# Cache loads on one ordered queue, a deeper K ring, and the output projection moved forward, in a decode kernel

## The chip, the cores and the metric

The kernel runs on one core of one Trainium2 chip. The metric is the device time of one execution in microseconds. A time is the median of several runs.

## The reference

One decode step for a batch of 2: attention of 16 query heads over a cache of 8 K/V heads with 32768 positions of 256 values, beside a small GELU feed-forward, mixed by a gate.

```python
q = (x @ wq).reshape(2, 1, 16, 256).transpose(0, 2, 1, 3)       # x is [2, 1, 448], bf16
k, v = repeat(k_cache, 2, axis=1), repeat(v_cache, 2, axis=1)   # caches [2, 8, 32768, 256], bf16
p = softmax(einsum("bhqd,bhkd->bhqk", q, k) / 16)
a = einsum("bhqk,bhkd->bhqd", p, v).transpose(0, 2, 1, 3).reshape(2, 1, 4096) @ wo
f = gelu(x @ w1 + b1) @ w2 + b2                                 # 448 -> 1792 -> 448
g = sigmoid((x * gate_w).sum(-1))
return g * a + (1 - g) * f
```

The two caches are 537 MB of the 547 MB that have to be read.

## The kernel before

There are 16 pairs (batch, K/V head), each with 16 K chunks and 16 V chunks of 1 MB (128 partitions x 16 tiles x 256). The scores of a whole pair are needed before its softmax, so the PV products of pair i run while the K chunks of pair i+1 are scored. A K chunk is transposed on the TensorE (PE) in four groups, copied out of PSUM by DVE or ACT, and multiplied by q; a V chunk takes 16 matmuls in four column groups, which leave four partial results.

K chunks live in a ring of NKB buffers and V chunks in a ring of NVB. SP issues K loads, ACT issues V loads, each on its own queue:

```python
def build_kernel(..., NKB=6, NVB=5, NKT=8, NTB=3, LAG=3):
    ...
    @block.sync
    def _(sp_):
        ...                                   # x, gate, biases; then all of wq, w1, w2
        for i in range(NP):
            for c in range(NCH):
                s, k = kslot(i, c)
                if k >= 1:
                    sp_.wait_ge(kfree[s], k)
                sp_.dma_start(knat[s][:, :, :], src).then_inc(kdma[s], 16)
        sp_.wait_ge(S["dve_fin"], 1)
        sp_.dma_start(out[:, 0, :], fin_bf[0:B, :])...
    ...
    def act_vtrig(i, c):                      # among ACT's other work, in order
        ...
        act.wait_ge(vfree[s], k)
        act.dma_start(vring[s][:, :, :], src).then_inc(vdma[s], 16)
```

The last pair's PV is followed by the combining of its four partials, a transpose, and the whole output projection in two halves of 224 columns:

```python
    def pe_attn_out(half):
        ...
        for h in range(HQ):
            for j in range(2):
                last = pe.matmul(ps[0:B, MB:MB + DHALF], lhsT=oT_bf[:, h, j, 0:B],
                                 rhs=wo_sb[:, h * 2 + j, half * DHALF:(half + 1) * DHALF], ...)
    def dve_a(half):
        ... tensor_copy(out=a_sb[half], in_=ps[0:B, MB:MB + DHALF])
        if half == 1:
            ... tensor_tensor(out=d1_sb, in0=a_sb, in1=f_sb, op=subtract)
            ... scalar_tensor_tensor(out=fin_bf, in0=d1_sb, scalar=g_sb, in1=f_sb, op0=mult, op1=add)
    ...
    ev(FIN, 4, "pe", "A0", pe_attn_out(0)); ev(FIN, 5, "dve", "A0r", dve_a(0))
    ev(FIN + 1, 4, "pe", "A1", pe_attn_out(1)); ev(FIN + 1, 5, "dve", "A1r", dve_a(1))
```

Of the kernel before, what the change touches and what calls it, by code (L numbers as in the profile page):

```python
# [4 lines left out]
ALU = mybir.AluOpType  # L5
# [49 lines left out]


def build_kernel(nc, A_x, A_k_cache, A_v_cache, A_wq, A_wo, B_x, B_w1, B_b1, B_w2, B_b2, gate_w, out,
                 NKB=6, NVB=5, NKT=8, NTB=3, LAG=3):
    B, _, D = A_x.shape
    _, HKV, SK, DH = A_k_cache.shape  # L60
    HQ = A_wq.shape[1] // DH
# [22 lines left out]
    def pair_bg(i):  # L84
        return i // HKV, i % HKV

    def drows(dc):
        return min(128, D - dc * 128)
# [80 lines left out]
    def kslot(i, c):  # L169
        gi = i * NCH + c  # L170
        return gi % NKB, gi // NKB

# [44 lines left out]
    with nc.Block() as block:  # L217
# [44 lines left out]
        def _(pool_):  # L262
# [7 lines left out]
            ch(pool_.memset(ones_f[:], 1.0))  # L270
            assert ch.n == POOL_DONE

        @block.sync
        def _(sp_):
            sp_.dma_start(x_bf[0:B, :], A_x[:, 0, :]).then_inc(S["ldA"], 16)
            sp_.dma_start(gw_bf[0:B, :], bass.AP(gate_w.tensor, gate_w.offset, [[0, B], [1, D]])).then_inc(S["ldA"], 16)
            sp_.dma_start(b2_bf[0:B, :], bass.AP(B_b2.tensor, B_b2.offset, [[0, B], [1, D]])).then_inc(S["ldA"], 16)
            sp_.dma_start(b1_sb[0:NFC, :], B_b1.rearrange("(c p) -> c p", p=128)).then_inc(S["ldA"], 16)
            for dc in range(NDC):
                r = drows(dc)  # L280
                wqv = vring[dc][:, :, :].rearrange("p t d -> p (t d)")
                sp_.dma_start(wqv[0:r, :], A_wq[dc * 128:dc * 128 + r, :]).then_inc(S["ld_wq"], 16)
            for dc in range(NDC):
                r = drows(dc)
                sp_.dma_start(w1_sb[0:r, dc, :], B_w1[dc * 128:dc * 128 + r, :]).then_inc(S["ld_w1"], 16)
            sp_.dma_start(w2_sb[:, :, :], B_w2.rearrange("(c p) d -> p c d", p=128)).then_inc(S["ld_w2"], 16)
            for i in range(NP):
                b, g = pair_bg(i)
                for c in range(NCH):
                    s, k = kslot(i, c)  # L290
                    if k >= 1:
                        sp_.wait_ge(kfree[s], k)
                    src = A_k_cache[b, g, c * C:(c + 1) * C, :].rearrange("(p t) d -> p t d", p=128)
                    sp_.dma_start(knat[s][:, :, :], src).then_inc(kdma[s], 16)
            sp_.wait_ge(S["dve_fin"], 1)
            sp_.dma_start(out[:, 0, :], fin_bf[0:B, :]).then_inc(S["osem"], 16)
            sp_.wait_ge(S["osem"], 16)

        def pe_prologue():
            pe.wait_ge(S["pool_c"], POOL_DONE)  # L300
            pe.wait_ge(S["ldA"], 16 * N_LDA)
            pe.wait_ge(S["dve_init"], 1)
            misc_begin("XT")
            last = None
            for dc in range(NDC):
                r = drows(dc)
                col = MB + 2 * dc
                last = pe.matmul(ps[0:r, col:col + 2], lhsT=x_bf[0:B, dc * 128:dc * 128 + r],
                                 rhs=identb[0:B, 0:B], start=True, stop=True)
            misc_end(last)  # L310
            misc_begin("B1T")
            last = pe.matmul(ps[:, MB:MB + NFC], lhsT=b1_sb[0:NFC, 0:128], rhs=identb[0:NFC, 0:NFC],
                             start=True, stop=True)
            misc_end(last)
            misc_begin("Q")
            pe.wait_ge(S["ld_wq"], 16 * NDC)
            last = None
            for h in range(HQ):
                for j in range(2):
                    col = MB + (h * 2 + j) * 2  # L320
                    for dc in range(NDC):
                        r = drows(dc)
                        wqv = vring[dc][:, :, :].rearrange("p t d -> p (t d)")
                        last = pe.matmul(ps[:, col:col + 2],  # L324
                                         lhsT=wqv[0:r, h * DH + j * 128:h * DH + j * 128 + 128],
                                         rhs=xT_sb[0:r, dc, 0:B], start=(dc == 0), stop=(dc == NDC - 1))
            misc_end(last)
            misc_begin("HT")
            pe.wait_ge(S["ld_w1"], 16 * NDC)
            last = None  # L330
            for fc in range(NFC):
                for dc in range(NDC):
                    r = drows(dc)
                    last = pe.matmul(ps[:, MB + 2 * fc:MB + 2 * fc + 2],  # L334
                                     lhsT=w1_sb[0:r, dc, fc * 128:(fc + 1) * 128],
                                     rhs=xT_sb[0:r, dc, 0:B], start=(dc == 0), stop=(dc == NDC - 1))
            misc_end(last)
# [16 lines left out]
        def pe_attn_out(half):  # L354
# [16 lines left out]
                    pass  # L371
            return fn

        def pe_tr(n):
            def fn():
                i, rem = divmod(n, G)
# [4 lines left out]
                if n >= NTB:  # L381
# [3 lines left out]
                    else:  # L385
                        pe.wait_ge(S["ev_dve"], evac_count(m))
                tb = tbank(n)
                last = None
                for tl in range(4):
                    t = 4 * q + tl  # L390
                    for j in range(2):
                        blk = tl * 2 + j
                        last = pe.transpose(tb[:, blk * 128:(blk + 1) * 128],  # L393
                                            knat[s][:, t, j * 128:(j + 1) * 128], identb[:, :])
                if evac_eng(n) == "act":
                    v = tr_act.inc(last)
                    assert v == evac_count(n)
                else:
                    v = tr_dve.inc(last)
                    assert v == evac_count(n)  # L400
# [13 lines left out]
        def pe_qk(n):  # L414
            def fn():
# [17 lines left out]
                for tl in range(4):  # L433
                    t = 4 * q + tl
                    col = base + (c * T + t) * 2
                    for j in range(2):
# [3 lines left out]
                                         start=(j == 0), stop=(j == 1))  # L440
                        if first is None:
                            first = last
                if pending_kfree:
                    assert len(pending_kfree) == 1
                    first.then_inc(kfree[pending_kfree.pop()], 1)
                last.then_inc(ktfree[slot], 1)
# [214 lines left out]
                                             in1=f_sb[0:B, :], op0=ALU.mult, op1=ALU.add).then_inc(S["dve_fin"], 1)  # L661
            return fn

        def act_vtrig(i, c):
            def fn():
                b, g = pair_bg(i)
                s, k = vslot(i, c)
                if k >= 1:
                    act.wait_ge(vfree[s], k)
                elif s < NWQ:  # L670
                    act.wait_ge(S["pe_misc"], misc_k("Q") + 1)
                src = A_v_cache[b, g, c * C:(c + 1) * C, :].rearrange("(p t) d -> p t d", p=128)
                act.dma_start(vring[s][:, :, :], src).then_inc(vdma[s], 16)  # L673
            return fn

        def act_wo():
            act.dma_start(wo_sb[:, :, :], A_wo.rearrange("(c p) d -> p c d", p=128)).then_inc(S["ld_wo"], 16)

        def act_gate():
            act.wait_ge(S["dve_gz"], 1)  # L680
# [19 lines left out]

        PRO = -1000
        ev(PRO, 0, "pe", "PRO", pe_prologue)
        misc_names.extend(["XT", "B1T", "Q", "HT"])
        ev(PRO - 1, 0, "dve", "INIT", dve_prologue_init)
        ev(PRO, 5, "dve", "XTr", dve_xt)
        ev(PRO, 6, "dve", "B1Tr", dve_b1t)
        ev(PRO, 7, "dve", "Qr", dve_q)
        ev(PRO, 8, "dve", "HTr", dve_ht)
        for i in range(NP):
            for c in range(NCH):  # L710
                a = vtrig_anchor(i, c)
                _, k = vslot(i, c)
                if k == 0:
                    ev(PRO + i * NCH + c, 12, "act", f"V{i},{c}", act_vtrig(i, c))
                else:
                    ev(a, 12, "act", f"V{i},{c}", act_vtrig(i, c))
        ev(PRO + NP * NCH + 1, 12, "act", "WO", act_wo)
        ev(PRO + NP * NCH + 2, 8, "act", "GATE", act_gate)
        ev(PRO + NP * NCH + 3, 8, "act", "GELUT", act_gelu_tanh)
        FA = min(8, NG)  # L720
        ev(FA, 5, "dve", "GELU2", dve_gelu2)
        ev(FA + 1, 4, "pe", "F0", pe_ffn_f(0))
        misc_F = [("F0", FA + 1), ("F1", FA + 2)]
        ev(FA + 1, 5, "dve", "F0r", dve_f(0))
        ev(FA + 2, 4, "pe", "F1", pe_ffn_f(1))
        ev(FA + 2, 5, "dve", "F1r", dve_f(1))
        for n in range(NG):
            ev(n, 0, "pe", f"tr{n}", pe_tr(n))
            if n % GPC == GPC - 1:
# [3 lines left out]
        for i in range(NP):  # L733
# [11 lines left out]
            ev(oc_anchor[i], 3, "dve", f"OC{i}", dve_ocomb_step(i))  # L745
            ev(oc_anchor[i] + 1, 4, "pe", f"OT{i}", pe_otr(i))
            ev(oc_anchor[i] + 1, 5, "dve", f"OTr{i}", dve_ot_step(i))
        ev(FIN, 4, "pe", "A0", pe_attn_out(0))
        ev(FIN, 5, "dve", "A0r", dve_a(0))
        ev(FIN + 1, 4, "pe", "A1", pe_attn_out(1))  # L750
        ev(FIN + 1, 5, "dve", "A1r", dve_a(1))

        events.sort(key=lambda e: (e[0], e[1], e[2]))
        for e in events:
            if e[3] == "pe" and (e[4].startswith(("TRM", "BC", "RS", "OT", "F0", "F1", "A0", "A1"))):
                misc_names.append(e[4])

        @block.tensor
        def _(pe_):
# [46 lines left out]
```

## Time and profile before

| | before |
|---|---|
| time, median of 4 runs | 1354.92 us (1354.38 to 1355.18) |
| span of the profiled run | 1353.1 us |
| HBM bytes read | 547.43 MB |
| PE busy | 78% |
| last V chunk landed | 1335.8 us |
| from there to the end | 17.3 us |

The page's queue table of the kernel before has packets, bytes and the share of the sixteen DMA engines' time, by queue. q1 is SP's queue, q10 is ACT's:

```profile
q1 hardware_dynamic: 39740, 275.34, 49.2%
q10 hardware_dynamic: 40976, 272.12, 49.1%
q8 instruction: 165, 2.70, 0.8%
```

Together the two load queues, q1 and q10, are 98% of the sixteen engines' time. The chain of waits on the same page, by engine, agrees:

```profile
DMA 78%; PE 16%; DVE 3%; issue 2%; ACTq 1%; ACT 0%; SPq 0%; DVEq 0%
```

The table by stretches of the kernel before: after the window and its length come PE, PE weight load, DVE, ACT and POOL busy time with instruction counts, the granted clock, the DMA share, and GB/s.

```profile
0.00:30.00 30.00, 15.09 (x202) 13.60 (x203) 2.86 (x11) 1.49 (x2) 1.41 (x9) 1.00 0.93 332
...
400.00:600.00 200.00, 160.67 (x3198) 142.94 (x3199) 80.93 (x137) 57.01 (x65) 0.00 (x0) 0.82 1.01 416
600.00:800.00 200.00, 158.30 (x3178) 142.21 (x3174) 78.84 (x128) 56.25 (x62) 0.00 (x0) 0.83 1.01 417
...
1270.00:1300.00 30.00, 23.41 (x492) 20.74 (x489) 13.55 (x24) 8.57 (x11) 0.00 (x0) 0.85 0.92 356
1308.00:1328.00 20.00, 8.18 (x128) 3.00 (x128) 0.00 (x0) 0.00 (x0) 0.00 (x0) 0.50 1.01 423
```

Mid-run the engines are full (share 1.01) at 416 to 417 GB/s, and PE is not. From 1308 to 1328 us only V's queue has work, and the rate is no lower. The list of waits of the kernel before (who waited for whom: us in total, times, longest) says which data PE runs out of:

```profile
PE ps L529 <- DMA vring<-in_A_v_cache_dram: 223.6, 197, 3.2
...
PE pst L393 <- DMA knat<-in_A_k_cache_dram: 2.0, 1, 2.0
```

It is V almost always. Last, the end of the timeline of the kernel before (start, duration, engine, line, operation; in brackets the idle time before it and what ended it):

```profile
1335.79 1.02 PE L529 MATMUL ps<-vring,p_sb 128*2 128x256 bf16 x16 [1.41 <-DMA vring<-in_A_v_cache_dram]
1336.87 0.41 DVE L636 COPY o_tmp<-ps 2x256 f32<-2x256 f32 x1 [35.99 <-PE ps L529]
1337.32 1.32 DVE L638 TENSOR_TENSOR o_tmp<-o_tmp,ps 2x256 f32<-2x256 f32 x3
1338.67 0.34 DVE L640 TENSOR_SCALAR o_sb<-o_tmp,rrec 2x256 f32<-2x256 f32 x1
...
1340.49 5.58 PE L365 MATMUL ps<-wo_sb,oT_bf 128*2 128x224 bf16 x32 [0.35 <-DVE oT_bf L649]
1346.10 0.38 DVE L656 COPY a_sb<-ps 2x224 f32<-2x224 f32 x1 [5.76 <-PE ps L365]
...
1346.54 3.23 PE L365 MATMUL ps<-wo_sb,oT_bf 128*2 128x224 bf16 x32 [0.47 <-DVE a_sb L656]
1349.80 0.38 DVE L656 COPY a_sb<-ps 2x224 f32<-2x224 f32 x1 [3.32 <-PE ps L365]
1350.21 0.61 DVE L659 TENSOR_TENSOR d_sb<-a_sb,f_sb 2x448 f32<-2x448 f32 x1
1350.86 0.67 DVE L660 SCALAR_TENSOR_TENSOR fin_bf<-d_sb,g_sb,f_sb 2x448 bf16<-2x448 f32 x1
```

No transfer of size runs here any more (0 GB/s from 1336 to 1340 us, 2 GB/s from 1340 to 1350). The step from 1340.5 to 1350.2 us is the output projection, and 14 of its 16 heads were ready 40 us earlier.

### The profile page before, as it was taken

To read this page: it belongs to the slowest core of one execution; us is meant where nothing else is said; L and a number is where in the kernel's file an instruction comes from. 1 tells how busy PE (TensorE), PEld (TensorE's weight loads), DVE (VectorE), ACT (ScalarE), POOL (GpSimd) and SP (SyncE) were. 2 spreads that over 40 slices of the span, in tenths; PEclk is the share of its full clock that TensorE was granted. 3 is DMA by queue.
4 is the path that set the end of the run, shared out by engine and by line. 5 is a ranking of instruction groups with operands and counts; after the bars stand their busy time and mean duration, and the time that the engine had idled before them with its cause. 6 is when DMAs were issued, how large, how long until landed. Compare 5 with 4: busy or idle time off the path is not lost.

```text
span 1353.1 us, 45118 instructions
## 1 busy us (share of the span) xinstructions
PE 1059.7 (78%) x20921; PEld 940.9 (70%) x20921; DVE 527.7 (39%) x890; ACT 367.3 (27%) x408; POOL 1.4 (0%) x9
## 2 busy tenths in 40 slices
PE   4986787878877887878787778788788878877865
PEld 4876676877767776767777677677677767777742
DVE  1553443434334343343434334343343434334321
ACT  0333232222323233232323223232232222222210
POOL 0000000000000000000000000000000000000000
PEclk9998987777888788788878878888788778878866
DMA  9999999999999999999999999999999999999994
GB/s 342 416 413 415 419 420 419 419 419 420 419 419 418 419 420 419 418 403 420 406 419 420 418 417 401 420 415 420 415 404 420 407 419 420 419 419 416 387 381 169
DMA packets 80904, 550.36 MB, mean 407 GB/s; under 512 B 8388, under 2 KB 14284, under 8 KB 14732
## 3 DMA queue, kind: packets, MB, share of 16 engines
q1 hardware_dynamic: 39740, 275.34, 49.2%
q10 hardware_dynamic: 40976, 272.12, 49.1%
q8 instruction: 165, 2.70, 0.8%
q14 instruction: 23, 0.19, 0.0%
HBM read 547.43 MB, written 0.00 MB: 405 GB/s over the span
## 4 chain that ended last, share of the span: by engine, by line
DMA 78%; PE 16%; DVE 3%; issue 2%; ACTq 1%; ACT 0%; SPq 0%; DVEq 0%
DMA vring<-in_A_v_cache_dram 76%; PE pst L393 8%; PE ps L529 4%; PE ps L438 2%; DMA knat<-in_A_k_cache_dram 1%; DVE o_tmp L638 1%; DMA vring<-in_A_wq_dram 1%; ACTq L673 1%; PE ps L324 1%; PE ps L365 1%; PE ps L511 1%; DVE o_tmp L636 0%; PE ps L334 0%; DVE pm_sb L596 0%; DVE kT L471 0%
## 5 line engine op out<-in xcount | busy, mean ns | idle before, releaser
L393 PE MATMUL pst<-identb,knat 128*128 128x128 bf16 x8192 | 759.8, 247 | 18.9 <-ACT kT L468 8.2
L471 DVE COPY kT<-pst 128x1024 bf16<-128x1024 bf16 x683 | 465.7, 691 | 725.1 <-PE pst L393 723.6
L393 PEld LDWEIGHTS pst<-identb,knat 128*128 128x128 bf16 x8192 | 568.6, 111 | 86.4 <-issue 76.2
L468 ACT ACTIVATE kT<-pst 128x1024 bf16<-128x1024 bf16 x341 | 349.2, 1024 | 844.9 <-PE pst L393 833.9
L438 PE MATMUL ps<-qT_sb,kT 128*128 128x2 bf16 x8192 | 367.8, 166 | 3.0 <-issue 2.0
L529 PE MATMUL ps<-vring,p_sb 128*2 128x256 bf16 x4096 | 184.8, 307 | 225.5 <-DMA vring<-in_A_v_cache_dram 223.6
L438 PEld LDWEIGHTS ps<-qT_sb,kT 128*128 128x128 bf16 x8192 | 347.5, 102 | 4.5 <-issue 4.5
L529 PEld LDWEIGHTS ps<-vring,p_sb 128*2 128x2 bf16 x4096 | 80.6, 87 | 267.5 <-DMA vring<-in_A_v_cache_dram 250.2
L695 ACT ACTIVATE p_sb<-ps,nb_sb 128x256 bf16<-128x256 f32 x32 | 16.5, 542 | 56.5 <-DVE nb_sb L615 56.5
L511 PE MATMUL ps<-identf,o_sb 2*128 2x2 f32 x64 | 13.0, 303 | 20.2 <-DVE nb_sb L615 17.8
L511 PEld LDWEIGHTS ps<-identf,o_sb 2*128 2x128 f32 x64 | 11.6, 253 | 21.8 <-DVE nb_sb L615 19.0
L636 DVE COPY o_tmp<-ps 2x256 f32<-2x256 f32 x16 | 6.5, 406 | 38.2 <-PE ps L529 38.2
L638 DVE TENSOR_TENSOR o_tmp<-o_tmp,ps 2x256 f32<-2x256 f32 x48 | 20.0, 416 | 1.7
L324 PE MATMUL ps<-xT_sb,vring 128*128 128x2 bf16 (+1 forms) x128 | 9.2, 174 | 10.8 <-DMA vring<-in_A_wq_dram 10.8
L324 PEld LDWEIGHTS ps<-xT_sb,vring 128*128 128x128 bf16 (+1 forms) x128 | 8.3, 106 | 11.8 <-issue 10.9
L481 PE MATMUL ps<-identf,pm_sb 128*2 128x128 f32 x32 | 6.6, 290 | 6.2 <-DVE pm_sb L596 6.2
L596 DVE TENSOR_REDUCE pm_sb<-ps 128x2 f32<-128x512 f32 x16 | 10.9, 680 | 0.9 <-PE ps L438 0.9
L365 PE MATMUL ps<-wo_sb,oT_bf 128*2 128x224 bf16 x64 | 8.8, 312 | 0.8 <-DVE a_sb L656 0.5
L681 ACT ACT_TABLE_LOAD x1 | 1.3, 1283 | 27.0 <-issue 27.0
L365 PEld LDWEIGHTS ps<-wo_sb,oT_bf 128*2 128x2 bf16 x64 | 6.3, 101 | 3.1 <-DVE a_sb L656 0.7
L554 DVE CAST qT_sb<-ps 128x64 bf16<-128x64 f32 x1 | 0.4, 435 | 19.9 <-PE ps L324 19.9
L490 PE MATMUL ps<-dg_sb,ones_f 2*128 2x2 f32 x32 | 7.1, 288 | 0.2 <-DVE dg_sb L605 0.2
(45 smaller groups left out, 62.7 us busy)
## 6 DMA issues: line engine op xcount, KB each, us to landing
knat<-in_A_k_cache_dram SPq DMA_DIRECT2D x256, 1024.0 KB, 20.8
vring<-in_A_v_cache_dram ACTq DMA_DIRECT2D x256, 1024.0 KB, 23.5
wo_sb<-in_A_wo_dram ACTq DMA_DIRECT2D x1, 3584.0 KB, 86.7
vring<-in_A_wq_dram SPq DMA_DIRECT2D x3, 1024.0 KB, 6.9
w_sb<-in_B_w_dram SPq DMA_DIRECT2D x1, 1568.0 KB, 17.2
w_sb<-in_B_w_dram SPq DMA_DIRECT2D x3, 448.0 KB, 12.1
vring<-in_A_wq_dram SPq DMA_DIRECT2D x1, 512.0 KB, 11.4
w_sb<-in_B_w_dram SPq DMA_DIRECT2D x1, 224.0 KB, 13.7
```

The costliest lines, as they stand in the source:

```text
L324: last = pe.matmul(ps[:, col:col + 2], lhsT=wqv[0:r, h * DH + j * 128:h * DH + j * 128 + 128], rhs=xT_sb[0:r, dc, 0:B], start=(dc == 0), s ...
L365: last = pe.matmul(ps[0:B, MB:MB + DHALF], lhsT=oT_bf[:, h, j, 0:B], rhs=wo_sb[:, h * 2 + j, half * DHALF:(half + 1) * DHALF], start=(k2 = ...
L393: last = pe.transpose(tb[:, blk * 128:(blk + 1) * 128], knat[s][:, t, j * 128:(j + 1) * 128], identb[:, :])
L438: last = pe.matmul(ps[:, col:col + 2], lhsT=kT[slot][:, blk * 128:(blk + 1) * 128], rhs=qT_sb[:, b, j, REP * g:REP * g + 2], start=(j == 0 ...
L468: ins = act.activation(out=kT[slot][:, :], in_=tbank(n), func=ACT.Copy)
L471: ins = dve.tensor_copy(out=kT[slot][:, :], in_=tbank(n))
L511: last = pe.matmul(ps[:, MB + 2 * j:MB + 2 * j + 2], lhsT=o_sb[0:2, si, j * 128:(j + 1) * 128], rhs=identf[0:2, 0:2], start=True, stop=True)
L529: last = pe.matmul(ps[32 * gq:32 * gq + 2, base:base + 256], lhsT=p_sb[:, i, (c * T + t) * 2:(c * T + t) * 2 + 2], rhs=vring[s][:, t, :], ...
L596: v = dve_pm.inc(dve.tensor_reduce(out=pm_sb[:, 2 * si:2 * si + 2], in_=scv, axis=AX.X, op=ALU.max))
L638: dch(dve.tensor_tensor(out=o_tmp[0:2, :], in0=o_tmp[0:2, :], in1=ps[32 * gq:32 * gq + 2, base:base + 256], op=ALU.add))
L673: act.dma_start(vring[s][:, :, :], src).then_inc(vdma[s], 16)
L695: v = act_exp.inc(act.activation(out=pv[:, m, :], in_=scv[:, m, :], func=ACT.Exp, bias=nb_sb[:, 2 * si + m:2 * si + m + 1], scale=SCALE, a ...
```

## The change

Its intent is threefold: to give K and V one order of loading that follows the order in which PE frees their buffers, with two more K buffers; to take work out of the start; and to take the output projection out of the end. Cut to its core:

```diff
-                 NKB=6, NVB=5, NKT=8, NTB=3, LAG=3):
+                 NKB=8, NVB=5, NKT=8, NTB=3, LAG=3):
...
+        # one job per K and V chunk; "a" is the step at which its buffer comes free
+        early = [j for j in jobs if j["a"] is None]
+        late = [j for j in jobs if j["a"] is not None]
+        late.sort(key=lambda j: (j["a"], j["u"]))
+        for j in early + late:
+            q = "sp" if load["sp"] <= load["act"] else "act"
+            if j["a"] is not None:
+                q = "sp"                      # all of the steady state on SP's queue
...
-            for dc in range(NDC): ...         # wq, w1, w2, then all K loads, on SP
+            for dc in WQ_SP:                  # half of wq on SP, half on ACT
+                load_wq(sp_, dc)
+            ...                               # then the jobs; w1, w2 after the eighth; wo on ACT
...
-        ev(PRO, 7, "dve", "Qr", dve_q)        # Q, HT and the FFN leave the prologue
+        ev(QA, 4, "pe", "Q", pe_q)
+        ev(HA, 4, "pe", "HT", pe_ht)
...
-        ev(FIN, 4, "pe", "A0", pe_attn_out(0))
-        ...
+        for h in range(HQ - REP):             # 14 heads, one after each of the last pair's V chunks
+            ev(pv_anchor(NP - 1, 1 + h), 12, "pe", f"PA{h}", pe_ap(h))
+        ev(FIN, 4, "pe", "PF", pe_af)         # the last pair's two heads: 4 matmuls, 448 wide
+        ev(FIN, 5, "dve", "PFr", dve_af)      # reads the result from PSUM, no copies
```

The release of a K buffer also moves, from the next score matmuls to the next transposes.

## The prediction

> **What bounds the kernel now.** The DMA engines. By the page's queue table the two load queues take 49.2% and 49.1% of the sixteen engines' span, 550.36 MB. The chain of waits is 78% DMA, 76% loads of V. The table by stretches shows 412 to 419 GB/s at a DMA share of 1.00 to 1.02 in every stretch from 30 to 1250 us. PE is busy 78%; its own waits are almost all for V (223.6 us), slack that the transfers leave.
>
> The last V chunk lands at 1335.8 us. At the mid-run pace of about 416 GB/s, 550 MB take 1323 us, and transfers start at about 3.4 us; the small-row weights (278 to 369 GB/s at 14 to 20 us) and a dip at 1276 to 1296 us (about 316 to 356) account for most of the rest. So almost nothing idles before 1335.8 us. The remaining tail is 17.3 us: PV 1.05, combining four PV partials 2.3, transposing the result and waits 1.3, the output projection in two halves 9.7 (1340.5 to 1350.2), two DVE steps 1.3, store and end 1.6.
>
> **What the change does.**
> 1. 28 of the 32 projection products, now 448 wide, move between the PV chunks of the last pair, where PE waits 1.4 us of every 2.48 us for V. After the last V only 4 remain. A 224-wide one takes 0.174 us there (5.58/32), so 4 of double width are about 1.4 us (estimate), without the copies between halves. **-8.3 us, all on the critical path.**
> 2. All steady K and V loads go on SP's queue in one order. No bandwidth gained: at 1308 to 1328 us only the V queue works, at 420 to 426 GB/s, as much as two together.[...] The waits follow PE's order of releases, so I expect no head-of-line loss: 0 to +2 us.
> 3. K buffers 6 to 8. PE waited only 2 us for K; the V ring of 5 limits. But K ends sooner, leaving V alone with 5 chunks in flight across the last softmax (about 7 us without a release): 0 to +2 us.
> 4. Wq first on both queues, HT and FFN out of the prologue, W1/W2 deferred: the dip at 12 to 20 us is partly filled: -1 us at most, since bytes bound this stage.
> 5. V issues leave ACT, where one blocks 10.8 us at 96.6 us in the chain; off the bound, 0.
> 6. The K release moves to the next transposes: 0.
>
> **Prediction: 1346 us**, range 1340 to 1351; faster by over 2%: 0.03, within 2%: 0.94, slower by over 2%: 0.03.
>
> **What would show it.** Last V landing at 1334 to 1338 us; from there to the end about 9 us; the two projection halves gone from the end of the timeline. ACT's queue down to a dozen issues, SP's near 97% of the engines' span. Mid-run 414 to 420 GB/s, share 1.0. PE still waiting 200 us or more for V, next to nothing for K; V's issue to landing still about 22 us.
>
> **What would make it wrong.** If the single ordered queue starves the engines (share under 0.97 mid-run), or SP's wait for Q (about 27 us) leaves a hole at 30 to 60 us, it is slower. If mid-run dips such as 575 to 585 us (349 to 377 GB/s) come from order or buffer depth and go, up to 9 us (1250 us at 416 instead of 419.5) more is gained: about 1337. If the last softmax starves V, the end dip grows and eats part of the gain.

## More of the kernel before

Each experiment ran in one job, on one chip, with runs of the kernel before, and its ratio is formed against those.

## The result, and the profile after

The changed kernel takes 1345.66 us (median of 9 runs, 1345.27 to 1346.60) against 1354.50 us (13 runs) of the kernel before: ratio 0.9934, 95% interval 0.9925 to 0.9944. Here and below a ratio is the mean time of one kernel's runs over that of the other's runs of the same rounds, so it is not quite the ratio of the medians quoted. The profiled span fell from 1353.1 to 1343.5 us, by 9.6 us.

The queue table of the changed kernel:

```profile
q1 hardware_dynamic: 75804, 538.03, 97.1%
q10 hardware_dynamic: 4912, 9.44, 2.0%
q8 instruction: 164, 2.69, 0.8%
```

The traffic has moved to one queue as intended, and it takes the same engine time: 99.1% of a span that is 0.7% shorter. The same stretches:

```profile
0.00:30.00 30.00, 6.76 (x81) 6.26 (x81) 2.74 (x7) 2.51 (x3) 1.41 (x9) 1.00 0.96 365
...
400.00:600.00 200.00, 157.97 (x3177) 142.09 (x3178) 80.88 (x137) 56.37 (x64) 0.00 (x0) 0.84 1.01 419
600.00:800.00 200.00, 161.35 (x3170) 145.00 (x3169) 78.17 (x127) 56.32 (x61) 0.00 (x0) 0.80 1.01 417
...
1270.00:1300.00 30.00, 24.17 (x507) 21.20 (x502) 13.71 (x25) 9.27 (x12) 0.00 (x0) 0.81 0.91 338
1308.00:1328.00 20.00, 12.46 (x150) 4.71 (x144) 0.00 (x0) 0.00 (x0) 0.00 (x0) 0.66 1.01 422
```

The start is fuller (365 instead of 332 GB/s), the dip before the last softmax is a little deeper (338 instead of 356), and the middle is what it was: the mean of all 5 us windows from 25 to 1275 us is 415.9 GB/s, against 416.3 before. The waits of the changed kernel:

```profile
PE ps L637 <- DMA vring<-in_A_v_cache_dram: 221.8, 195, 3.2
...
PE pst L496 <- DMA knat<-in_A_k_cache_dram: 24.3, 2, 14.7
```

PE still waits for V in the middle. Its two waits for K stand at the start: 14.7 us until 23.8 us, for the first K load, and 9.6 us until 68.3 us. Before the second, SP had stood 16.1 us at one V issue (39.6 to 55.7 us), and the K loads in line behind that issue went out late. And the end:

```profile
1334.70 0.61 PE L637 MATMUL ps<-vring,p_sb 128*2 128x256 bf16 x16 [0.99 <-DMA vring<-in_A_v_cache_dram]
1335.36 0.41 DVE L744 COPY o_tmp<-ps 2x256 f32<-2x256 f32 x1 [35.05 <-PE ps L637]
1335.81 1.32 DVE L746 TENSOR_TENSOR o_tmp<-o_tmp,ps 2x256 f32<-2x256 f32 x3
1337.16 0.34 DVE L748 TENSOR_SCALAR o_sb<-o_tmp,rrec 2x256 f32<-2x256 f32 x1
...
1338.88 1.65 PE L466 MATMUL ps<-wo_sb,oT_bf 128*2 128x448 bf16 x4 [0.26 <-DVE oT_bf L757]
...
1340.57 0.61 DVE L472 TENSOR_TENSOR d_sb<-ps,f_sb 2x448 f32<-2x448 f32 x1 [1.74 <-PE ps L466]
1341.22 0.67 DVE L473 SCALAR_TENSOR_TENSOR fin_bf<-d_sb,g_sb,f_sb 2x448 bf16<-2x448 f32 x1
```

The last V lands at 1334.7 us, 1.1 us earlier, and 8.8 us follow it instead of 17.3. So 8.5 us of the 9.6 come from behind the last transfer.

The trace also holds the completion time of every 1 MB cache load, and the n-th completion of one kernel can be set against the n-th of the other. This is worked out from the completion records, not a view of the profile:

```
cache load, from 0        10     40    100    250    400    490    511
before, us              54.8  139.0  292.6  674.0 1055.4 1283.2 1335.8
after, us               46.9  137.0  290.5  672.1 1053.4 1281.2 1334.7
difference               7.9    2.0    2.0    2.0    2.0    2.0    1.1
```

Up to load 10 the order of the weights differs. The columns from load 40 to 490 are loads that land second of a K and a V load. Their difference is 1.8 to 2.1 us in 217 of 226 cases, so over 1.1 ms the loads land at the same pace. The loads between them differ by 2.7 to 4.4 us, because before the change the two loads of a pair land 0.1 to 1.8 us apart and after it about 2.5 us. By all bytes landed, the changed kernel leads by 1.0 us from 60 to 200 MB, by 2.4 to 3.6 us from 250 to 525 MB, and by 1.1 us at 540 MB, after the dip before the last softmax. So both counts leave 1.1 us at the end, and both lose in the dip, but whether the start gained 1 or 2 us depends on the count, and each kernel has one profile.

### The profile page after: what moved, and what is told of

Same layout as the page of the kernel before. It is cut to its first block, busy times and chain, and to the rows that moved or that the text cites. A ratio compares the mean times of both kernels' runs of the same rounds, so it can differ in the third digit from the quotient of the medians.

```text
span 1343.5 us, 45053 instructions
## 1 busy us (share of the span) xinstructions
PE 1047.1 (78%) x20889; PEld 929.6 (69%) x20889; DVE 526.4 (39%) x888; ACT 367.5 (27%) x408; POOL 1.4 (0%) x9
## 3 DMA queue, kind: packets, MB, share of 16 engines
q1 hardware_dynamic: 75804, 538.03, 97.1%
## 4 chain that ended last, share of the span: by engine, by line
DMA 80%; PE 14%; DVE 2%; SPq 2%; issue 2%; ACT 0%; DVEq 0%
DMA vring<-in_A_v_cache_dram 78%; PE pst L496 7%; PE ps L637 4%; DMA knat<-in_A_k_cache_dram 2%; PE ps L546 2%; SPq L328 1%; DVE o_tmp L746 1%; PE ps L397 1%; PE ps L619 1%; DVE pm_sb L704 0%; PE ps L409 0%; DVE o_tmp L744 0%; PE ps L589 0%; SPq L351 0%; PE ps L466 0%
## 5 line engine op out<-in xcount | busy, mean ns | idle before, releaser
L496 PE MATMUL pst<-identb,knat 128*128 128x128 bf16 x8192 | 751.7, 246 | 26.9 <-DMA knat<-in_A_k_cache_dram 24.3
L496 PEld LDWEIGHTS pst<-identb,knat 128*128 128x128 bf16 x8192 | 562.3, 110 | 94.4 <-issue 65.3
L637 PE MATMUL ps<-vring,p_sb 128*2 128x256 bf16 x4096 | 182.1, 303 | 222.9 <-DMA vring<-in_A_v_cache_dram 221.8
L619 PEld LDWEIGHTS ps<-identf,o_sb 2*128 2x128 f32 x64 | 11.1, 243 | 22.8 <-DVE nb_sb L723 20.2
L457 PE MATMUL ps<-wo_sb,oT_bf 128*2 128x448 bf16 x28 | 11.3, 500 | 0.0
L598 PEld LDWEIGHTS ps<-dg_sb,ones_f 2*128 2x128 f32 x32 | 5.6, 219 | 0.8 <-DVE dg_sb L713 0.5
## 6 DMA issues: line engine op xcount, KB each, us to landing
vring<-in_A_v_cache_dram SPq DMA_DIRECT2D x256, 1024.0 KB, 24.1
```

Source lines behind the costliest of these rows:

```text
L457: pe.matmul(ps[0:B, SC[0]:SC[0] + D], lhsT=oT_bf[:, h, j, 0:B], rhs=wo_sb[:, h * 2 + j, :], start=(h == 0 and j == 0), stop=False)
L496: last = pe.transpose(tb[:, blk * 128:(blk + 1) * 128], knat[s][:, t, j * 128:(j + 1) * 128], identb[:, :])
L598: ins = pe.matmul(ps[:, MB:MB + 2], lhsT=ones_f[0:2, 0:128], rhs=dg_sb[0:2, 2 * si:2 * si + 2], start=True, stop=True)
L619: last = pe.matmul(ps[:, MB + 2 * j:MB + 2 * j + 2], lhsT=o_sb[0:2, si, j * 128:(j + 1) * 128], rhs=identf[0:2, 0:2], start=True, stop=True)
L637: last = pe.matmul(ps[32 * gq:32 * gq + 2, base:base + 256], lhsT=p_sb[:, i, (c * T + t) * 2:(c * T + t) * 2 + 2], rhs=vring[s][:, t, :], ...
```

## The experiments

The theory under test (A) is: the transfers run at a pace that neither queue, order nor K depth touches, and the change gains what it takes from behind the last V, with 1 to 2 us from the start. The first rival (B) credits the ordered queue and the deeper ring. Each experiment gave the correct result.

### The tail alone

The kernel before, with only the projection moved:

```diff
# against the kernel before
-        ev(FIN, 4, "pe", "A0", pe_attn_out(0)) ... dve_a(1)
+        for h in range(HQ - REP):
+            ev(pv_anchor(NP - 1, 1 + h), 12, "pe", f"PA{h}", pe_ap(h))
+        ev(FIN, 4, "pe", "PF", pe_af); ev(FIN, 5, "dve", "PFr", dve_af)
```

> The kernel before, with only the output projection moved: 28 of its 32 products, 448 wide, run between the last pair's V chunks, and 4 stay behind the last V. Theory A (the change gains by its tail): the last V lands at 1335 to 1336.5 us as before, the tail after it falls from 17.3 to about 8.8 us, and the time is 8 to 9 us below before, ratio 0.9934 to 0.9941. Rival B (the ordered queue and the deeper K ring gain, the tail little): at most 3 us below before, ratio 0.998 or more.

Measured: 1346.56 us against 1355.66, ratio 0.9937 (0.9923 to 0.9950). The first matmul on the last V chunk, from its timeline:

```profile
1335.57 1.02 PE L556 MATMUL ps<-vring,p_sb 128*2 128x256 bf16 x16 [1.47 <-DMA vring<-in_A_v_cache_dram]
```

The span was 1344.7 us, so 9.2 us follow the last V. The tail alone gives nearly all of the gain; B is rejected.

### Everything but the tail

```diff
# against the changed kernel
-        for h in range(HQ - REP): ev(..., pe_ap(h)); ev(FIN, ..., pe_af); ev(FIN, ..., dve_af)
+        ev(FIN, 4, "pe", "A0", pe_attn_out(0)) ... dve_a(1)
```

> The changed kernel with the old projection at its end (two halves after the last V); queue order, 8 K buffers, start and K release stay as changed. Theory A: the last V lands at about 1334.7 us as in the changed kernel, the tail is 17.3 us again, ratio to before 0.998 to 1.000 (0 to 2 us gained by the start). Rival B: ratio 0.994 to 0.996, most of the gain remains.

Measured: 1353.73 us, ratio 0.9989 (0.9976 to 1.0001), last V at 1335.3 us, 16.9 us behind it. Queue, order, ring, start and release together are worth about 0.1%, which the interval (a gain of 0.24% to a loss of 0.01%) does not tell from nothing. The two parts add up: 0.63% and 0.11% against 0.66% for the whole change, within the intervals.

### V back on ACT's queue

```diff
# against the changed kernel
             if j["a"] is not None:
-                q = "sp"
+                q = "act" if j["kind"] == "V" else "sp"
```

> The changed kernel with the V loads of the steady state issued by ACT again, on ACT's queue, at the same places in the order of work; everything else as changed. Theory A (which queue carries a load is nothing to the sixteen engines): ratio to before 0.9925 to 0.9945, as the changed kernel, and mid-run about 416 GB/s. Rival B (one ordered queue is worth something): 2 us or more slower than the changed kernel, ratio 0.995 or more.

Measured: 1346.36 us, ratio 0.9933 (0.9921 to 0.9945), last V at 1335.3 us. Two queues or one is the same here, to the resolution of the runs. The queue tables of the two kernels fit this: the two load queues took 49.2% and 49.1% of the sixteen engines' time before, and after the change SP's queue alone took 97.1%.

### Six K buffers

```diff
# against the changed kernel
-                 NKB=8, NVB=5, ...
+                 NKB=6, NVB=5, ...
```

> The changed kernel with 6 K buffers instead of 8. Theory A: V's ring of 5 holds the pace, so ratio to before 0.9925 to 0.9945, equal to the changed kernel; PE waits for K stay under 30 us in total and the end dip before the last softmax is smaller (K ends later). Rival B (the two added buffers absorb stalls): 2 us or more slower than the changed kernel, and more waits for K.

Measured: 1346.92 us, ratio 0.9938 (0.9926 to 0.9950). PE's waits for K rose from 24.3 to 34.8 us, in 12 places instead of 2, a little over the 30 us expected; the last V landed at 1336.8 us. The difference of 0.0004 to the changed kernel is inside both intervals; by the medians, from different jobs, it is 1.3 us, and whether the two buffers are worth that stays open. The dip before the last softmax was expected to be smaller, and it was not: 332 GB/s from 1270 to 1300 us, against 338 with eight buffers and 356 before the change. So the two added buffers are not what deepened it.

### A deeper V ring

Rival C asks whether the dips in the middle and at the end come from too few V chunks in flight.

```diff
# against the changed kernel
-                 NKB=8, NVB=5, ...
+                 NKB=6, NVB=7, ...
```

> The changed kernel with 6 K and 7 V buffers (the same 13 chunks). PE's waits are for V alone, so if depth in flight limited the transfers, this is where depth would pay. Theory A (eight of the sixteen DMA engines, which end each transfer last by 14 to 18 us from 550 us on, never idle and set the end): the last V lands at 1334 to 1336 us again, ratio to before 0.9925 to 0.9945, and the spread of the completions of one load only grows. Rival C (the mid-run dips and the dip before the last softmax come from too few V chunks in flight): mid-run rises to 419 GB/s, the last V lands 5 us or more earlier, ratio 0.990 or less.

Measured: 1346.34 us, ratio 0.9941 (0.9928 to 0.9953), last V at 1336.8 us (0.8 us later than expected). Against the run above, with the same six K buffers (0.9938), only the V ring differs. From 200 to 1250 us the rate was 418 GB/s against 417 in the changed kernel, and the largest spread of one load's completions rose from 19.1 to 20.2 us. C is rejected. The waits of this run are worth reading against those shown above:

```profile
PE pst L496 <- DMA knat<-in_A_k_cache_dram: 222.8, 182, 17.2
...
PE ps L637 <- DMA vring<-in_A_v_cache_dram: 10.7, 11, 2.3
```

PE now waits 222.8 us for K and 10.7 us for V, with much the same sum (233.5 against 246.1) and the same time. The name in a list of waits told which ring was shorter, not what bounded the kernel.

### What the transfers' pace hangs on: the sixteen completions of one load

The trace has sixteen completion records for each of the 512 cache loads. They are read here as one from each of the sixteen engines. That is the author's reading, since the records do not say which engine is which; under it, their order shows how far the engines are apart. From the changed kernel, for loads that ended at these times, in us before the last of the sixteen (worked out from the records):

```
ended at   the eight earliest                          the eight latest
 119.7    -3.5 -3.4 -3.3 -3.3 -3.1 -3.1 -2.4 -2.2     -2.0 -1.9 -1.9 -1.5 -0.5 -0.4 -0.3 0.0
 405.4   -11.3-11.2-11.1-11.1-10.9-10.2 -9.5 -7.1     -2.1 -2.1 -2.0 -1.9 -1.8 -1.8 -1.5 0.0
 831.5   -17.4-17.4-17.3-17.3-16.7-16.5-16.5-12.3     -1.7 -1.4 -0.7 -0.6 -0.5 -0.5 -0.2 0.0
1329.8    -4.0 -3.9 -3.9 -3.9 -3.9 -3.9 -3.8 -3.4     -2.3 -1.9 -1.5 -1.4 -0.6 -0.5 -0.3 0.0
```

At 405 us eight completions stand apart from the other eight, and at 831 us they are 12 to 17 us before the last one. That they are the same eight engines each time is argued, since the records name none. PE waits for all sixteen of a chunk (`wait_ge(kdma[s], 16 * (k + 1))`), so it starts on a chunk only after the last. Theory A, in its second form, says that the fast eight run ahead until they have no more work and then idle, that this makes the mid-run dips, and that the slow eight set the end. Instruction fetches were my suspect for the slowness, since the page shows 164 of them, of 16 KB each, and each takes about 1.07 us of an engine in the packet records (175.6 us in all).

The first test adds instructions that do nothing, on an engine that is busy for 1.4 us in all:

```diff
# against the changed kernel, on POOL, after its setup
+            for _k in range(8000):
+                pool_.engine_nop()
```

> The changed kernel with 8000 empty instructions on POOL, which is otherwise idle; nothing waits for them. They add about 0.5 MB, some 31 fetches of 16 KB, to the 164 of the instruction queue; one fetch takes about 1.07 us of one DMA engine. Theory A with its cause (instruction fetches land on eight of the sixteen engines, and these eight set the end): 31 times 1.07 over 8 is +4 us, ratio about 0.9965, spread of completions larger by up to 4 us. If fetches were even over sixteen engines: +2 us, spread unchanged. Rival D (fetches are nothing to the time): ratio 0.9925 to 0.9945.

Measured: 1368.37 us, ratio 1.0100 (1.0086 to 1.0114), 22.7 us over the changed kernel (medians of different jobs). Every size in the expectation was wrong. The queue table of this run shows where the fetches went:

```profile
q8 instruction: 164, 2.69, 0.8%
q14 instruction: 86, 0.70, 0.1%
```

Queue 14 had 23 packets in the changed kernel, so 63 were added, of 8 KB each. Half a megabyte (0.70 MB against 0.19) in 550 is 0.1% of the bytes and cost 1.7% of the time. The completions show how (loads counted from 0 again):

```
ended at   first fifteen of sixteen, us before the last    n-th load later than in the changed kernel
 134.5    -14.7 to -13.2                                     17.9 (load 40, at 154.9 us)
 215.2    -22.9 to -22.5                                     26.2 (load 70, at 240.8 us)
 297.3    -22.7 to -20.3                                     37.2 (load 100, at 327.7 us)
 509.0    -15.5 to -11.4                                     32.5 (load 190, at 551.2 us)
 996.3    -15.9 to  0.0                                      21.3 (load 370, at 998.8 us)
   -      -                                                  23.0 (load 511, at 1357.6 us)
```

One completion alone falls behind, so by the same reading one engine alone got the added fetches; it lost 37.2 us to 63 of them, 0.59 us each. The other fifteen ran up to some 23 us ahead of it, presumably as far as the loads in flight allow, and came no further ahead after that (22.5 to 22.9 us at 215 us, 20.3 to 22.7 at 297). The fifteenth completion shows what they lost: set against the last one of the same load in the changed kernel, it was 2.1 us late at load 60, 22.2 at load 130, and 21 to 23 from there to the end. From load 100 on the delay of the lone engine melted by 15.9 us until, near 1000 us, the usual slow engines had caught up with it (seven completions early, nine late, so it was one of the fast eight); from there the delay is 21 to 23 us. So, by this reading, the pace of this kernel is that of the slowest engine, and a fast engine has slack that the slow eight use up at 15.9/671, about 2.4 us per 100 us.

That reading makes an odd claim that can be tested: half of the instructions must cost far less than half.

```diff
-            for _k in range(8000):
+            for _k in range(4000):
```

> The changed kernel with 4000 empty POOL instructions instead of 8000. With 8000 the 63 added fetches of 8 KB all fell, in the first 330 us, to one engine, which came 37.2 us behind its time in the changed kernel (0.59 us a fetch), more than the 22.6 us by which the other fifteen could run ahead; the end was 23 us late. Theory A (the pace is that of the slowest engine; one of the otherwise fast engines has slack, which the eight slow ones use up in the course of the run, at about 2.3 us per 100 us): 32 fetches put one engine about 18 us behind by 170 us, the others never run out of work, from there the delay melts away and is 0 to 4 us at the last V; ratio to before 0.9925 to 0.997. Rival (fetches cost in proportion): half of 23 us, +11 us on the changed kernel, ratio about 1.002.

Measured: 1349.12 us, ratio 0.9956 (0.9943 to 0.9970). Queue 14 had 54 packets, 31 more than in the changed kernel. Load 40 was 16.9 us late, load 190 9.1, load 280 3.2, the last 3.4. The cost is 3.5 us by the medians and not 11; the proportional rival is rejected, and the slowest-engine reading holds. The others were not left wholly untouched: from load 70 on the fifteenth completion was 3.2 us late or more, and that is what remains at the end.

### Shifting bytes between the halves: two attempts that did not answer

If half of the engines idle, bytes could be moved to them. Four K chunks were loaded by sixteen transfers of 8 rows. That this gives one half of the engines more to do than the other was the author's assumption, not shown before the run:

```diff
# against the changed kernel; BAL is chunks 50, 100, 150, 200
+                if i * NCH + c in BAL:
+                    for r in range(16):
+                        eng.dma_start(knat[s_][8 * r:8 * r + 8, :, :], src[8 * r:8 * r + 8]).then_inc(kdma[s_], 16)
```

> The changed kernel with 4 of the 256 K chunks loaded by sixteen transfers of 8 rows each[...]. Theory A (one half is the bound, the other half idles some 15 to 20 us in all): if the half that gets more is the idle one, the last V lands 7 to 10 us earlier, ratio about 0.987; if it is the bound one, it lands 8 to 10 us later, ratio about 1.000. Rival (all sixteen are equally the bound, dips come from order): later by 10 us in both cases only if engines are equal, and then the spread of completions would show no two groups.

Measured: 1381.94 us, ratio 1.0204 (1.0190 to 1.0218), beyond both outcomes. The sixteen transfers of one chunk posted 128 late completions, eight each, which is read as eight engines each; but they were spread over 17.7 us in the first of the four chunks, and over 24 to 29 us in the others, where by estimate 5 us of transfer stood on each engine (1 MB over eight engines is 16 packets of 8 KB for each, at the 0.31 us that such a packet takes in the packet records). So the run priced something else. A rival that was not tested is the issuing: SP took 6.4 us to issue the sixteen transfers of the first chunk, where a whole load takes 0.33 us, and then 2 to 4 us for most of its issues up to 249 us. The second attempt took rows 4 partitions apart:

```diff
-                        eng.dma_start(knat[s_][8 * r:8 * r + 8, :, :], src[8 * r:8 * r + 8])...
+                        p0 = 32 * (r % 4) + r // 4
+                        eng.dma_start(knat[s_][p0:p0 + 29:4, :, :], src[p0:p0 + 29:4])...
```

> The experiment with four shifted chunks again, now with rows that lie 4 partitions apart in each of the sixteen small transfers, because in the first form (8 neighbouring rows each) one such chunk took 17.7 us from its first to its last completion where 5 us of transfer stood on each of eight engines, which spoils its verdict. Theory A (half of the engines are the bound): if neighbouring rows were the trouble, one chunk's completions now spread over 6 us or less, and the last V lands 5 to 10 us earlier than in the changed kernel if the eight engines used are the idle half (ratio 0.986 to 0.990), or 8 to 10 us later if they are the bound half (ratio about 1.000). If the rows' places were not the trouble: ratio 1.015 or more again.

Measured: 1373.61 us, ratio 1.0137 (1.0121 to 1.0154). The first chunk's completions still spread over 17.0 us (22 to 24 in the others) and this form was only 8.3 us faster, so the rows' places were not the main trouble. SP's sixteen issues took 11.2 us. In the packet records the 8 KB packets during that time took 0.37 to 0.54 us (medians of 3 us windows from 232 to 247 us) against 0.31 us otherwise, and the rate fell to 268 to 306 GB/s. Why, and which half is the slow one, stays open.

### A shorter tail

Theory A says that every microsecond taken from behind the last V is one of the time. For the last pair, the four PV partials are copied in one step and summed, scaled and transposed by one matmul pair against a selection matrix that holds 1/rowsum, prepared before the last V; and the mix uses a precomputed (1-g)f.

```diff
# against the changed kernel, last pair only
-   o_tmp = ps[0:2]; o_tmp += ps[32:34]; += ps[64:66]; += ps[96:98]; o = o_tmp * rrec; transpose by identity
+   dve.tensor_copy(out=o98[0:98, 0:256], in_=ps[0:98, base:base + 256])
+   pe.matmul(ps[:, MB + 2*j:MB + 2*j + 2], lhsT=o98[0:98, j*128:(j+1)*128], rhs=sel[0:98, 0:2], ...)
-   d = a - f; fin = d * g + f
+   dve.scalar_tensor_tensor(out=fin_bf, in0=ps[...], scalar=g_sb, in1=f2_sb, op0=mult, op1=add)   # f2 = f - g*f
```

> The changed kernel with a shorter tail after the last V: the four PV partials of the last pair are copied in one step and summed, scaled and transposed by one matmul pair against a selection matrix scaled beforehand (three adds of 0.44 us and one scaling of 0.34 us go), and the gate's mix is one DVE step instead of two (0.62 us goes). Theory A (every us taken from behind the last V is a us of time): tail from 8.8 to about 6.5 us, ratio to before 0.9910 to 0.9930, 2.2 us below the changed kernel. Rival: hidden, no difference from the changed kernel.

Measured: 1343.36 us against 1354.76, ratio 0.9917 (0.9903 to 0.9931). The end of its timeline:

```profile
1334.66 1.02 PE L655 MATMUL ps<-vring,p_sb 128*2 128x256 bf16 x16 [0.70 <-DMA vring<-in_A_v_cache_dram]
1335.73 0.42 DVE L787 COPY junk<-ps 98x256 f32<-98x256 f32 x1 [33.49 <-PE ps L655]
...
1336.31 0.98 PE L634 MATMUL ps<-sel,junk 98*128 98x2 f32 x4 [0.62 <-DVE junk L787]
...
1339.24 0.67 DVE L477 SCALAR_TENSOR_TENSOR fin_bf<-ps,g_sb,a_sb 2x448 bf16<-2x448 f32 x1 [1.75 <-PE ps L471]
```

The last V landed as before, 6.8 us follow it instead of 8.8 (span 1341.5 us), and the time is 2.3 us lower by medians. Its ratio interval overlaps that of the changed kernel, so the size rests on the timeline. By the medians this is the fastest of all versions run.

## Why the prediction was right, point by point

- **The time.** 1346 us predicted, 1345.66 measured. The terms, 8.3 and 1 us off and 0 to 4 us on, allow 1345.6 to 1349.6 us; the number stood near the low end, and it fits so closely because both allowances for losses came out near zero.
- **Point 1, the tail: right.** -8.3 us predicted; the tail went from 17.3 to 8.8 us. The four products of double width took 1.65 us, not the estimated 1.4. The tail alone (ratio 0.9937) and all but the tail (0.9989) show it twice.
- **Point 2, one ordered queue: right.** Putting V back on ACT's queue changed nothing (0.9933 against 0.9934). "No head-of-line loss" holds for the time and not for PE: the wait of 9.6 us for K behind SP's long V issue is gone with V on ACT's queue, where one wait for K is left (14.7 us). It cost no time that the runs show.
- **Point 3, the K ring: right in size, its reason not borne out.** The dip before the last softmax grew (338 instead of 356 GB/s), with a loss of 0.9 us by the loads' table, inside the 0 to 2 foreseen. But it is as deep with six K buffers (332), so K's earlier end through the two added buffers is not its cause; which part of the new loading is stays open. That V's ring limits was a reading of the waits and too strong: with a deeper V ring and a smaller K ring the wait stood at K, and the time stayed.
- **Point 4, the start: about right.** At most 1 us was allowed; 1.1 us is left at the last load, and the start itself gained 1.0 us by bytes or 2.0 by the loads' table. Q came later than thought, too: the V loads that wait for it were issued from 35.6 us, not 27, because Q's matmuls now run behind the first transposes. No idle hole followed, since K and the weights kept the engines busy (share 1.05 from 30 to 60 us), but the rate there was 387 GB/s against 417 before.
- **Points 5 and 6: consistent with zero** as parts of the 0.9989. V back on ACT's queue undoes points 2 and 5 together and changed nothing; point 6 was not tried alone.
- **What would show it.** V landed at 1334.7 us (1334 to 1338 foreseen); SP's queue took 97.1% (near 97); ACT's queue had 7 issues (a dozen); mid-run 415 to 419 GB/s; V took 24.1 us from issue to landing, where "still about 22" was said and the page of the kernel before has 23.5. The wait for K, "next to nothing", was 24.3 us, two waits at the start.
- **"Almost nothing idles" was right for the engines that count, by the reading above.** The open alternative, 9 us more if the dips go with order or depth, did not come: the dips did not go with the new order, with V on ACT's queue or with seven V buffers. The dips (in the changed kernel a DMA share of 0.90 and 344 GB/s from 660 to 665 us, for one) are consistent with fast engines idling while the slow eight work; that the slowest engine sets the pace is, by that reading, what the added instructions show (63 fetches, one completion behind, 22.7 us). That fetches are what slows the eight is argued, not shown: 175.6 us over eight engines is 22 us in 1340, about 1.6 us per 100 us, while the runs show about 2.4.

## What to carry to other kernels

When the transfers are saturated, find the moment the last load lands: what stood behind it was paid in full here (8.5 of the 9.6 us came from there, and 2.0 us less in the shorter tail were 2.3 us of time), and work that does not need that load belongs in front of it. In this kernel the list of waits named the shorter ring and not the bound, and the change of the rings that only swapped the name was worth nothing. Look at the spread of one load's completions before you trust a mean DMA share: here it was 1.01 mid-run while the completions of one load lay up to 19.1 us apart, and 8000 instructions that do nothing, by 63 fetches of 8 KB, lengthened the kernel by 22.7 us.
